# Attention and feed-forward in one kernel: the order of each engine's queue written down as a table

## The chip, the cores and the metric

The kernel runs on one core of one Trainium2 chip. The metric is the device time of one launch in microseconds (us). Before the change it was 1242.29 us, the median of three runs (1240.87 to 1242.33).

## The reference, cut to what matters

Attention over 8 batches of 8 heads, 576 tokens, 64 columns a head, with a block-causal mask of 64x64 blocks. Its output is reshaped to 4608 tokens of 512 columns and goes through a feed-forward part with a hidden width of 2048:

```python
scores = scale * np.matmul(q, k.transpose(0, 1, 3, 2))      # scale = 1/8
scores = np.where(block_i >= block_j, scores, -1000000000.0)
attn = softmax(scores);  x = attn @ v  ->  (4608, 512)
h = x @ w_in                                                 # 512 x 2048
g = np.where(h >= 1, h, np.where(h <= -1, 0.0, (h + 1) ** 2 / 4))
out = g @ w_out                                              # 2048 x 512
```

All inputs and the output are float32.

## The kernel before, in words

**Precision.** Nearly every operand of TensorE is split into a high and a low word of a rounded float32 format, and a product is the sum of three matmuls (high by high, high by low, low by high). That is why one `ffn_in` issues 12 matmuls (L777) and one `ffn_out` 12 (L801, L806), and why the scores are two matmuls a tile (L484 and L487), where the tiles `ka`/`qa` and `kb`/`qb` hold both words. `ka` and `qa` also hold four rows that make the mask; these are written by VectorE into a small tile `mrow` (L134 to L138) and sent into `qa` and `ka` by four DMAs (L150, L151).

**Attention.** There are 32 pairs (batch, two heads). A pair is a generator of eight steps; a step issues one group of scores (`scores`, `scores_last`), the turning of an earlier group of probabilities (`turn`), a piece of the product with v (`attn_v`), and a piece of the next pair's preparation. A group of scores is: matmuls into a PSUM bank `ps_s` (L484, L487); a row maximum on VectorE (`nm`, L508; L533 and L537 for the last group); the exponential on ScalarE (L513, L539); one over the sum on VectorE (`sm`, L494, L495); a multiplication on VectorE (`pr`, L519; L548 for the last group). `turn` then transposes the probabilities on TensorE (L559 or L561, into `ps_t`), in the first batch straight from `pr`, later from a copy that a DMA makes (L247, L251), which here lies in unused ends of `xl` or `vsr`. The next pair's q and k are split on VectorE and GpSimd (`qs` L353 and L354, `ks` L365 and L366) and transposed (L424) in the first two batches; later pairs take another path (L403).

**Weights.** The two weight matrices come in 32 pieces of 512 KB into tiles `bits` (L165) and are split by a helper `convert`: two operations on ScalarE (L170, L171), three on VectorE (L172, L175, L178), one on GpSimd (L184), one on ScalarE (L186), one on GpSimd (L188). `w_in` stays in SBUF, `w_out` goes back to memory in split form.

**Feed-forward.** Nine chunks of 512 tokens by 16 slices of 128 hidden columns. Its steps begin after 36 attention steps, one for each further attention step, and run alone at the end. A slice is 12 matmuls into the only bank `ph` (L777), the activation on ScalarE and VectorE (L786, L787, L790), the split of g (L791 on ScalarE, L792 on GpSimd), and 12 matmuls into four banks `po` (L801, L806).

**What sets the order.** The program text says which step issues what, and each tile comes from a pool that hands out its buffers in turn (3 banks `work`, 1 `ph`, 4 `po`; 2 or 3 buffers for most SBUF tiles, 6 for the small ones). The order in which the instructions stand in the queue of each engine, and in that of the SP queue which issues the DMAs, is decided by the ordering tool when the program is built. An engine then takes its queue strictly from the front: an instruction that waits holds up all that stand behind it.

## Time and profile before

| | |
|---|---|
| median of three runs | 1242.29 us |
| the profiled execution | 1239.06 us |
| its span, first to last instruction | 1237.3 us |
| TensorE busy | 1186.6 us, 96% |
| VectorE busy | 863.8 us, 70% |
| ScalarE busy | 698.5 us, 56% |
| GpSimd busy | 371.8 us, 30% |
| mean granted TensorE clock | 0.989 |

The profiled execution is 3.2 us (0.26%) under the median. In the rows of the profile PE is TensorE, PEld its weight loads, DVE VectorE, ACT ScalarE, POOL GpSimd and SPq the queue that issues DMAs. A row of a timeline is: start in us, duration, engine, line, operation, output<-inputs, shape; in brackets the idle time of the engine ahead of it and what ended that. A row of a stretch is: the stretch, its length, the busy time and the instructions of each engine, the granted TensorE clock (1.00 is full rate, 0.50 half), the DMA share and GB/s.

### The profile page before, as it was taken

The page shows a single profiled execution, that of the slowest core. Times are in us where ns is not written, and L with a number is a line of the kernel's source. Part 1 is how long each engine was busy: PE and PEld are TensorE (multiplying, and loading weights), DVE is VectorE, ACT ScalarE, POOL GpSimd, SP SyncE. Part 2 cuts the span into 40 slices and gives each one's busy share as a digit, 9 for nine tenths or more (in the row PEclk, how much of TensorE's full clock was granted, in tenths as well). Part 3 has the DMA queues.
Part 4 walks back from the last instruction along what each step waited for, and adds up shares of the span by engine and source line. Part 5 has one row for each costly group of instructions (what it writes and reads, how often), then busy time and mean ns, then how long its engine had stood idle before and what let it go on. Part 6 is the DMA issues. An engine that isn't in the chain of part 4 may idle for free.

```text
span 1237.3 us, 19822 instructions
## 1 busy us (share of the span) xinstructions
PE 1186.6 (96%) x6280; PEld 993.1 (80%) x6280; DVE 863.8 (70%) x2124; ACT 698.5 (56%) x1731; POOL 371.8 (30%) x366
## 2 busy tenths in 40 slices
PE   4878898999999999999999999999999999999998
PEld 3666677788888888888888888888888888888886
DVE  8888778658777877787777877787778776322322
ACT  5877667546566656665666665666566654222222
POOL 3444546312222222222222222222222222222222
PEclk9988998999999999999999999999999999999999
DMA  5756776778986655565555555565556443333332
GB/s 165 213 176 208 235 247 221 225 202 255 291 270 219 192 162 156 147 198 166 163 159 180 164 160 160 148 196 151 155 149 192 142 135 111 119 102 102 120 103 102
DMA packets 177192, 215.40 MB, mean 174 GB/s; under 512 B 109872, under 2 KB 128304, under 8 KB 176320
## 3 DMA queue, kind: packets, MB, share of 16 engines
q1 hardware_dynamic: 177088, 214.14, 56.1%
q8 instruction: 50, 0.82, 0.3%
q14 instruction: 54, 0.44, 0.1%
HBM read 134.74 MB, written 31.98 MB: 135 GB/s over the span
## 4 chain that ended last, share of the span: by engine, by line
PE 86%; DVE 5%; DMA 4%; ACT 2%; issue 2%; POOL 1%; SPq 0%; ACTq 0%; DVEq 0%; POOLq 0%
PE ph L777 31%; PE po L801 20%; PE po L806 10%; PE ps_av L598 9%; PE ps_s L484 5%; PE ps_s L487 4%; PE ps_t L559 4%; PE ps_qk L403 1%; DMA bits<-in_moe_w_in_dram 1%; DVE bits L172 1%; POOL bits L184 1%; PE ps_t L561 1%; DVE nm L508 1%; DVE bits L178 1%; DVE shifted L175 1%
## 5 line engine op out<-in xcount | busy, mean ns | idle before, releaser
L792 POOL TENSOR_TENSOR gl<-t,gh 128x512 fp32r<-128x512 f32 x144 | 186.5, 1295 | 522.8 <-ACT gh L791 338.2
L801 PE MATMUL po<-wo,gh 128*128 128x512 f32 x1152 | 294.1, 396 | 0.1
L801 PEld LDWEIGHTS po<-wo,gh 128*128 128x128 f32 x1152 | 211.2, 188 | 43.3 <-ACT gh L791 0.6
L777 PE MATMUL ph<-xh,wih 128*128 128x512 f32 x576 | 232.7, 404 | 0.4 <-DVE t L790 0.4
L777 PE MATMUL ph<-xh,wil 128*128 128x512 f32 x576 | 228.1, 396 | 0.0
L777 PE MATMUL ph<-xl,wih 128*128 128x512 f32 x576 | 226.9, 394 | 0.0
L787 DVE SCALAR_TENSOR_TENSOR t<-t 128x512 f32<-128x512 f32 x144 | 101.0, 701 | 161.5 <-ACT t L786 158.6
L786 ACT ACTIVATE t<-ph 128x512 f32<-128x512 f32 x144 | 86.2, 599 | 160.5 <-PE ph L777 160.5
L791 ACT CAST gh<-t 128x512 fp32r<-128x512 f32 x144 | 89.4, 621 | 118.9 <-DVE t L790 118.8
L806 PE MATMUL po<-wo,gl 128*128 128x512 f32 x576 | 155.3, 391 | 0.0
L484 PE MATMUL ps_s<-ka,qa 68*128 68x288 f32 (+4 forms) x384 | 133.8, 363 | 4.9 <-DMA ka<-mrow 4.0
L513 ACT ACTIVATE pr<-ps_s,nm 128x128 f32<-128x128 f32 x192 | 100.4, 525 | 57.5 <-DVE nm L508 56.4
L508 DVE TENSOR_REDUCE nm<-ps_s 128x1 f32<-128x128 f32 (+3 forms) x256 | 118.9, 482 | 16.4 <-PE ps_s L487 15.6
L777 PEld LDWEIGHTS ph<-xh,wil 128*128 128x128 f32 x576 | 109.1, 189 | 24.0
L806 PEld LDWEIGHTS po<-wo,gl 128*128 128x128 f32 x576 | 108.0, 188 | 22.9
L777 PEld LDWEIGHTS ph<-xl,wih 128*128 128x128 f32 x576 | 109.6, 190 | 19.3
L777 PEld LDWEIGHTS ph<-xh,wih 128*128 128x128 f32 x576 | 109.2, 190 | 19.3 <-DVE t L790 0.8
L381 POOL TENSOR_TENSOR vsr<-vn,vsr 64x64 fp32r<-64x64 f32 (+1 forms) x96 | 56.5, 589 | 227.1 <-ACT vsr L380 226.0
L487 PE MATMUL ps_s<-kb,qb 128*128 128x288 f32 (+4 forms) x384 | 120.4, 321 | 0.0
L790 DVE TENSOR_TENSOR t<-ph,t 128x512 f32<-128x512 f32 x144 | 98.7, 685 | 2.0
L559 PEld LDWEIGHTS ps_t<-ident_r,prr 128*128 128x128 f32 x600 | 68.5, 139 | 22.4 <-issue 0.5
L494 DVE TENSOR_SCALAR sm<-sm 128x1 f32<-128x1 f32 x256 | 38.5, 151 | 65.0 <-ACT pr L513 54.8
(115 smaller groups left out, 1879.7 us busy)
## 6 DMA issues: line engine op xcount, KB each, us to landing
wo<-wo_split SPq DMA_DIRECT2D x144, 512.0 KB, 3.4
prr<-pr SPq DMA_DIRECT2D x96, 192.0 KB, 3.0
prr<-pr SPq DMA_DIRECT2D x48, 256.0 KB, 2.8
out_dram<-ob SPq DMA_DIRECT2D x36, 256.0 KB, 2.9
bits<-in_moe_w_in_dram SPq DMA_DIRECT2D x16, 512.0 KB, 4.6
bits<-in_moe_w_out_dram SPq DMA_DIRECT2D x16, 512.0 KB, 4.0
wo_split<-ws SPq DMA_DIRECT2D x16, 512.0 KB, 2.9
qa<-qb SPq DMA_DIRECT2D x63, 128.0 KB, 2.4
```

Of the source, the lines that this page charges most:

```text
L484: nc.tensor.matmul(ps, qa[:KA, j, c0 : c0 + P], ka[:KA, j, k0 : k0 + n], start=first, stop=False)
L487: nc.tensor.matmul(ps, qb[:, j, c0 : c0 + P], kb[:, j, k0 : k0 + n], start=False, stop=last)
L508: nc.vector.tensor_reduce(out=nm[:, i : i + 1], in_=ps[:, cs], axis=AX.X, op=ALU.max, negate=True)
L513: nc.scalar.activation(raw[:, cs], ps[:, cs], AF.Exp, bias=nm[:, i : i + 1], scale=1.0, accum_out=sm[:, i : i + 1],)
L559: nc.tensor.transpose(out.bitcast(F32R), src, ident_r)
L598: nc.tensor.matmul(ps[:, lo_col:], vt, x, start=first and i == 0 and m == 0, stop=last and i == len(parts) - 1 and m == len(mov) - 1,)
L777: nc.tensor.matmul(ph, w[:, cc, fs], x[:, cc, xs], start=(cc == 0 and i == 0), stop=(cc == NCC - 1 and i == 2),)
L787: nc.vector.scalar_tensor_tensor(out=t_, in0=t_, scalar=1.0, in1=t_, op0=ALU.min, op1=ALU.mult)
L790: nc.vector.tensor_tensor(out=t_, in0=ph, in1=t_, op=ALU.max)
L792: nc.gpsimd.tensor_tensor(out=gl, in0=t_, in1=gh.bitcast(F32), op=ALU.subtract)
L801: nc.tensor.matmul(po[tt], gh[:, ts_], wo[:, w, :], start=(fc == 0 and w == 0), stop=False)
L806: nc.tensor.matmul(po[tt], gl[:, ts_], wo[:, 0, :], start=False, stop=fc == NFC - 1)
```

## The change

Two things are written into the program as tables. `SLOTS` names the buffer that each tile gets: pools have one buffer for each tag, and a helper `slot` adds the next digit of the table to the tag, so that the buffers "t0" and "t1" stand for what were two buffers of "t". `QUEUES` holds, for each of the five queues, a list of numbers (packed and written as text). At the end of the kernel all instructions of an engine are put into the order of its list, and a dependence without a semaphore is laid from each to the next, which fixes the order:

```diff
+SLOTS = {
+    "nat": (
+        '0210210210210210210210210210210210210210'
+    ),
...
+QUEUES = {
...
+    "Pool": (
+        'c-qa6;SPWx2!uhz)%(A29AZ$v-3pe(xATxr2)<ADvqg#}Q8$Jvp5RM^UQ6Fh+no&iPNRp_=?tDO8n>lPpDHQd<lf7j<A2pu='
...
-    att2 = ctx.enter_context(tc.tile_pool(name="att2", bufs=3))
+    att2 = ctx.enter_context(tc.tile_pool(name="att2", bufs=1))
...
+    turns = {tag: iter(x) for tag, x in SLOTS.items()}
+
+    def slot(pool, shape, dtype, tag, name):
+        return pool.tile(shape, dtype, tag=tag + next(turns[tag]), name=name)
...
-            pr = att3.tile([P, S], F32, tag="pr", name="pr")
+            pr = slot(att3, [P, S], F32, "pr", "pr")
...
+    emitted = [
+        x for x in nc.cur_bb.bb.instructions
+        if not isinstance(x, (mybir.BassTilePoolBoundary, mybir.InstRegisterMove))
+    ]
+    for engine, table in QUEUES.items():
+        left = [x for x in emitted if str(x.engine).rsplit(".", 1)[-1] == engine]
+        queue = [left.pop(n) for n in array("H", zlib.decompress(base64.b85decode(table)))]
+        for before, after in zip(queue, queue[1:]):
+            tc.add_manual_dep(
+                after, before.name,
+                mybir.DependencyInfo(mybir.DependencyClass.NoSync, mybir.DependencyReason.DATA),
+                reason="queue",
+            )
```

The instructions are the same ones on every engine: 6170 on TensorE, 2126 on VectorE, 1413 on ScalarE, 371 on GpSimd, 952 in the SP queue. Which tile shares a buffer with which is also the same, up to the buffers' names. Only the order differs, and only in the front part of each queue: on TensorE among the first 1808 instructions (1524 of them stand at another place, none further than 35 places up or 26 down), on VectorE among the first 785 (540 moved, up to 13 places), on ScalarE among the first 524 (397), on GpSimd among the first 156 (95), in the SP queue among the first 412 (369, up to 39 places). In the trace of before this is about the first 400 us. The lines of the changed kernel are numbered anew: its L484 is now L597, L487 L600, L777 L890, L559 L672, L424 L537, L365 L478, L172 L285, L508 L621, L519 L632, L787 L900, L790 L903, L165 L278, L150 and L151 L263 and L264, L336 and L341 L449 and L454, L317 and L320 L430 and L433. Three places are shown; the numbers behind the names tell tiles of one name apart.

**The SP queue at the start.** `qn` and `kn` are q and k of the first pair, `vs` its v, `bits` pieces of the weights, `mrow` the rows of the mask. Before, from the row of k's last blocks on:

```order
L341 DMA kn<-in_k_dram 64x64 x2
L317 DMA vs<-in_v_dram 128x4x64
L320 DMA vs<-in_v_dram 64x64
L317 DMA vs<-in_v_dram 128x4x64
L320 DMA vs<-in_v_dram 64x64
L165 DMA bits<-in_moe_w_in_dram 128x1024 x2
L150 DMA qa<-mrow 4x576
L151 DMA ka<-mrow 4x576
L150 DMA qa<-mrow 4x576
L151 DMA ka<-mrow 4x576
```

In the changed kernel, from the same row on:

```order
L454 DMA kn<-in_k_dram 64x64 x2
L278 DMA bits<-in_moe_w_in_dram 128x1024 x2
L264 DMA ka<-mrow 4x576
L263 DMA qa<-mrow 4x576
L454 DMA qn<-in_q_dram 64x64
L433 DMA vs<-in_v_dram 64x64 x2
L548 DMA qa<-qb 64x512
L278 DMA bits<-in_moe_w_in_dram 128x1024
L449 DMA qn<-in_q_dram 128x2x256
L263 DMA qa<-mrow 4x576
L548 DMA ka<-kb 64x512
```

The four loads of v moved behind the weights and behind the mask rows of the first head, and the mask rows of the second head moved further back.

**TensorE at about 125 us.** `ph_1514` is a slice of the feed-forward, `ps_t_1450` the transposes of a group of probabilities that a DMA has put into `xl`. Before:

```order
L424 MATMUL ps_qk_1396<-ident_r_92,ks_1317 128x128 x4
L777 MATMUL ph_1514<-xh_94,wih_96 128x512
L484 MATMUL ps_s_1438<-ka_103,qa_101 128x512
L487 MATMUL ps_s_1438<-kb_104,qb_102 128x512
L777 MATMUL ph_1514<-xl_95,wih_96 128x512
L777 MATMUL ph_1514<-xh_94,wil_97 128x512
L559 MATMUL ps_t_1450<-ident_r_92,xl_95 128x128 x3
```

In the changed kernel:

```order
L537 MATMUL ps_qk_1396<-ident_r_92,ks_1317 128x128
L597 MATMUL ps_s_1438<-ka_103,qa_101 128x512
L890 MATMUL ph_1514<-xl_95,wih_96 128x512
L890 MATMUL ph_1514<-xh_94,wil_97 128x512
L600 MATMUL ps_s_1438<-kb_104,qb_102 128x512
L890 MATMUL ph_1514<-xh_94,wih_96 128x512
L890 MATMUL ph_1514<-xl_95,wih_96 128x512
L890 MATMUL ph_1514<-xh_94,wil_97 128x512
L672 MATMUL ps_t_1450<-ident_r_92,xl_95 128x128 x3
```

Three more matmuls of `ph_1514` now stand ahead of the transposes.

**VectorE at about 185 us.** `ks_2229` is a later pair's k, `bits_2083` a piece of the weights, `nm_2119`, `sm_2120` and `pr_2118` one group of probabilities, `t_2103` a slice's activation. Before:

```order
L354 SCALAR_TENSOR_TENSOR qs_2192<-qn_2184,qs_2192 128x9x64
L365 CAST ks_2229<-kn_2188 128x8x64
L365 CAST ks_2229<-kn_2188 128x64
L634 TENSOR_TENSOR xl_95<-ps_av_2066,xh_94 128x320
L172 TENSOR_SCALAR bits_2083<-bits_2083 128x512
L175 TENSOR_SCALAR shifted_202<-bits_2083 128x512
L178 SCALAR_TENSOR_TENSOR bits_2083<-bits_2083,shifted_202 128x512
L787 SCALAR_TENSOR_TENSOR t_2103<-t_2103 128x512
L508 TENSOR_REDUCE nm_2119<-ps_s_2117 128x1
L790 TENSOR_TENSOR t_2103<-ph_2090,t_2103 128x512
```

In the changed kernel:

```order
L478 CAST ks_2229<-kn_2188 128x8x64
L467 SCALAR_TENSOR_TENSOR qs_2192<-qn_2184,qs_2192 128x9x64
L572 CAST ka_103<-ps_qk_2057 64x2x64
L285 TENSOR_SCALAR bits_2083<-bits_2083 128x512
L288 TENSOR_SCALAR shifted_202<-bits_2083 128x512
L291 SCALAR_TENSOR_TENSOR bits_2083<-bits_2083,shifted_202 128x512
L747 TENSOR_TENSOR xl_95<-ps_av_2066,xh_94 128x320
L621 TENSOR_REDUCE nm_2119<-ps_s_2117 128x1
L900 SCALAR_TENSOR_TENSOR t_2103<-t_2103 128x512
L903 TENSOR_TENSOR t_2103<-ph_2090,t_2103 128x512
```

The short cast `ks_2229` of 128x64 is no longer in this stretch: it stands 13 places earlier in the queue, right behind the two L632 of `pr_1984`; and the row maximum `nm_2119` has moved ahead of L900.

## The prediction

> **What bounds the kernel now.** I read the page's busy times first, then the busy time in five stretches, and after that the chain of waits and the timeline at the places of TensorE's waits. The stretches come early because the change reaches only the front part of the queues.

> ```profile
> PE 1186.6 (96%) x6280; PEld 993.1 (80%) x6280; DVE 863.8 (70%) x2124; ACT 698.5 (56%) x1731; POOL 371.8 (30%) x366
> ```

> ```profile
> 0.00:20.00 20.00, 5.61 (x28) 4.73 (x29) 14.28 (x42) 8.56 (x19) 5.09 (x12) 1.00 0.66 191
> 20.00:70.00 50.00, 40.41 (x224) 32.73 (x222) 46.56 (x130) 40.24 (x104) 24.36 (x22) 1.00 0.62 188
> 70.00:150.00 80.00, 66.88 (x338) 53.52 (x339) 62.98 (x166) 57.05 (x144) 37.78 (x35) 0.87 0.67 206
> 150.00:250.00 100.00, 92.72 (x466) 73.78 (x465) 74.52 (x167) 63.74 (x148) 46.94 (x42) 0.97 0.73 232
> 250.00:1236.00 986.00, 981.03 (x5230) 828.37 (x5228) 665.47 (x1623) 528.87 (x1319) 257.61 (x256) 1.00 0.54 165
> ```

> TensorE bounds the whole. Its idle time is 20 - 5.61 = 14.4 us in the first stretch, then 9.6, 13.1 and 7.3, and from 250 us on 986 - 981.03 = 5.0. The work stays the same, so a new order can gain only from the 44.4 us of idle before 250 us, from a few of the last 5, and from the granted clock, which is 0.87 and 0.97 in two stretches. From 20 to 70 us VectorE is busy 46.56 of 50: there it sets the pace, and a better order of TensorE alone brings little.

> The clock falls in steps of about 3.4 us. These are stretches cut on that grid:

> ```profile
> 87.25:90.66 3.41, 2.30 (x16) 1.57 (x14) 3.38 (x10) 1.56 (x5) 0.21 (x2) 1.00 0.62 165
> 90.66:94.07 3.41, 1.00 (x6) 0.69 (x6) 2.58 (x8) 2.55 (x10) 2.32 (x2) 1.00 0.22 49
> 94.07:97.48 3.41, 1.59 (x10) 1.57 (x10) 3.41 (x12) 2.28 (x7) 2.31 (x2) 0.50 0.77 249
> 97.48:100.89 3.41, 3.41 (x14) 2.74 (x13) 2.32 (x9) 3.17 (x8) 1.55 (x2) 0.50 0.80 282
> 124.80:128.20 3.40, 0.77 (x6) 0.36 (x4) 2.07 (x4) 1.88 (x4) 0.80 (x1) 1.00 0.89 324
> 128.20:131.62 3.42, 3.42 (x13) 2.74 (x12) 1.15 (x4) 1.83 (x4) 1.28 (x2) 0.50 0.75 246
> 189.65:193.06 3.41, 1.67 (x11) 1.35 (x9) 2.29 (x6) 1.58 (x4) 2.22 (x2) 1.00 0.92 322
> 193.06:196.47 3.41, 2.44 (x8) 2.06 (x9) 2.38 (x7) 2.03 (x5) 1.66 (x2) 0.50 0.40 123
> 196.47:199.88 3.41, 3.41 (x11) 2.64 (x9) 2.71 (x6) 2.63 (x7) 1.50 (x2) 0.50 0.70 267
> ```

> Each spell at half rate follows a stretch in which TensorE was busy 1.67 of 3.41 us or less; the one with 2.30 was followed by none. The rate stays at half until a stretch was full (97.48, 128.20, 196.47). So a wait costs its own length, and then half of the time of the work that runs slowly.

> **The change part by part.** Buffers are shared as before, so the slot table costs nothing by itself. What counts is which waits stand ahead of which work, and I follow the places where TensorE waits.

> *The start.* The first scores wait for the mask rows in `ka`. Pieces of the chain, then of the timeline:

> ```profile
> 8.71 4.84 DMA ka<-mrow
> 13.69 0.45 PE ps_s L484
> ```

> ```profile
> 4.28 0.59 SPq L317 DMA_DIRECT2D vs<-in_v_dram  x1
> ...
> 6.66 1.06 SPq L165 DMA_DIRECT2D bits<-in_moe_w_in_dram  x2
> ...
> 9.23 0.69 DVE L431 CAST ka<-ps_qk 64x512 fp32r<-64x512 f32 x1
> ...
> 13.40 0.68 ACT L170 ACTIVATE bits<-bits 128x512 f32<-128x512 f32 x1 [1.08 <-DMA bits<-in_moe_w_in_dram]
> ```

> `ka<-mrow` landed at 8.71 + 4.84 = 13.55, right behind the second piece of the weights (13.40); both were issued after the loads of v. In the changed queue the weights begin where those loads stood, 6.66 - 4.28 = 2.4 us sooner, and VectorE fills `mrow` ahead of the splits of k. The first scores should begin at 13.69 - 2.4 = 11.3. They can't begin before L431 ends, 9.23 + 0.69 = 9.92, a gain of 3.8; and nothing is gained if the mask rows land no sooner. VectorE runs nearly full from there to 70 us, and L285 on a piece of weights now stands ahead of the first row maxima, so of the 2.4 I keep 2.0. The moved loads of v and the second head's mask rows are first used several microseconds after they now land. Bounds: 0 and 3.8.

> *27 to 74 us.* VectorE's rows are exchanged among themselves, some weight operations out of the way of a group of probabilities, some into it. I take 0, by bounds of 1 on both sides, the length of one or two of them.

> *92, 110 and 125 us.* Three waits of TensorE, each with what stands behind it:

> ```profile
> 95.89 1.30 PE L561 MATMUL ps_t<-ident_r,pr 128*128 128x128 f32 x5 [2.94 <-DVE sm L494]
> 96.84 0.81 PE L424 MATMUL ps_qk<-ident_r,ks 128*128 128x128 f32 x4
> 97.46 0.76 PE L484 MATMUL ps_s<-ka,qa 68*128 68x512 f32 x1
> ```

> ```profile
> 112.09 0.45 PE L559 MATMUL ps_t<-ident_r,xl 128*128 128x128 f32 x3 [1.45 <-DMA xl<-pr]
> 112.37 0.37 PE L484 MATMUL ps_s<-ka,qa 68*128 68x288 f32 x1
> 112.58 0.30 PE L487 MATMUL ps_s<-kb,qb 128*128 128x288 f32 x1
> 112.72 0.30 PE L484 MATMUL ps_s<-ka,qa 68*128 68x288 f32 x1
> ```

> ```profile
> 128.00 0.49 PE L559 MATMUL ps_t<-ident_r,xl 128*128 128x128 f32 x3 [2.63 <-ACT ps_s L513]
> ...
> 128.84 0.63 PE L777 MATMUL ph<-xl,wih 128*128 128x512 f32 x1
> 129.26 0.63 PE L777 MATMUL ph<-xh,wil 128*128 128x512 f32 x1
> ```

> At 92 us the changed queue puts the four L424 ahead of the L561 that wait: 97.46 - 96.84 = 0.6 us of work goes into the wait. On VectorE one weight operation leaves the way of the probabilities that are waited for, and others enter it; the next group's L519 comes ahead of a row maximum. I take 1.0; bounds 0 and the wait, 2.9. At 110 us two of the L484 and one L487 go ahead of the wait for the copied probabilities, 112.72 - 112.37 = 0.35 for two, 0.4 in all; bounds 0 and 1.45. At 125 us it is three L777, which start 129.26 - 128.84 = 0.42 apart at half rate: 3 x 0.42 = 1.3. TensorE's busy time in 124.80 to 128.20 goes from 0.77 to about 1.5 at full rate, still under 1.67, so I leave the spell at half rate behind it in place. If it goes too, another 3.42 / 2 = 1.7 is gained: bounds 0 and 3.0.

> *190 us.* TensorE, then VectorE, with the same pair of casts from the start for comparison:

> ```profile
> 194.03 0.62 PE L559 MATMUL ps_t<-ident_r,xl 128*128 128x128 f32 x3 [2.71 <-DVE pr L519]
> ```

> ```profile
> 5.51 0.62 DVE L365 CAST ks<-kn 128x512 fp32r<-128x512 f32 x2
> ...
> 181.14 0.43 DVE L172 TENSOR_SCALAR bits<-bits 128x512 f32<-128x512 f32 x1 [1.56 <-ACT bits L170]
> ...
> 184.71 2.25 DVE L365 CAST ks<-kn 128x512 fp32r<-128x512 f32 x2
> ...
> 189.86 0.68 DVE L787 SCALAR_TENSOR_TENSOR t<-t 128x512 f32<-128x512 f32 x1
> ```

> The wait of 2.71 ends with `pr_2118`, and the chain to it on VectorE begins with two casts that take 2.25 instead of 0.62, 1.6 more. The short one now stands in front of L172 where VectorE was idle 1.56, and the row maximum no longer waits for L787 (0.68). The chain comes 1.6 + 0.6 = 2.2 us sooner, and one L777 goes ahead of the wait. What is left of the 2.71 is 0.3 or so; the stretch is then busy over 2.30, and the spell at half rate should go: (2.44 + 3.41) / 2 = 2.9. Together 5.1, of which later waits, whose chains come only 2.2 sooner, take back part: I take 3.0; bounds 0 and 5.1. [...]

> *From 250 us.* TensorE is full, and some score matmuls are moved up as far as 21 places, ahead of others, although their bank comes free only with an exponential. Such a wait lasts at most about a row maximum and an exponential:

> ```profile
> L513 ACT ACTIVATE pr<-ps_s,nm 128x128 f32<-128x128 f32 x192 | 100.4, 525 | 57.5 <-DVE nm L508 56.4
> L508 DVE TENSOR_REDUCE nm<-ps_s 128x1 f32<-128x128 f32 (+3 forms) x256 | 118.9, 482 | 16.4 <-PE ps_s L487 15.6
> ```

> 0.525 + 0.482 = 1.0 us for each. I charge one, 1.0; bounds: all of the idle time of 5.0 gained, or the loss of the slower rival below.

> The sum: 2.0 + 0 + 1.0 + 0.4 + 1.3 + 3.0 - 1.0 = 6.7 us gained. The profiled execution would go from 1239.06 to 1232.4; it is 3.2 us under the median, so against the median of 1242.29 I forecast 1242.29 - 6.7 = 1235.6. A change of 0.2% (2.5 us) is about what a measurement of this kernel can tell from none.

> **The rivals.**

> *Given back, no change (0.17).* VectorE is busy 46.56 of 50 us before 70 us, so an earlier start may only become a longer wait for it, and the waits after 200 us may eat the rest: of the terms only 0.4 + 1.3 would stay, less 1.0: 0.7 gained, 1241.6. For it: VectorE's share. Against it: that share falls to 62.98 of 80 behind 70 us, and at 125 and 190 us VectorE stood idle too.

> *Slower, by new waits in the full part (0.13).* Each pair has one L444; from 250 to 400 us there are five, the first and the last at

> ```profile
> 259.15 0.22 PE L444 MATMUL ps_qk<-ident_r,qk 128*128 128x128 f32 x1
> ...
> 393.97 0.25 PE L444 MATMUL ps_qk<-ident_r,qk 128*128 128x128 f32 x1
> ```

> If in each pair three groups of scores wait 1.0 us, 15 us of TensorE's time is new idle; against gains of 6.7 + 1.0 = 7.7 that is 7.3 us lost, 1249.6. It decides from 7.7 + 2.5 = 10.2 us of new idle behind 250 us. For it: the strict order, and only 5.0 us of waits there now, which the change can hardly better. Against it: most of the moves are within work that is all ready.

> *Larger, because half rate goes nearly everywhere (0.12).* If the waits at 90.66 and 124.80 also shrink until their stretches are busy over 2.30, the spells behind them vanish: (1.59 + 3.41) / 2 + 3.42 / 2 = 4.2 more, and with the full 5.1 instead of 3.0 at 190 us, 2.1 more: 13.0 gained, 1229.3. Against it: what moves into those waits is 0.6 and 1.3 us.

> *The clock doesn't follow the waits (0.10).* If the rate falls for another cause, the spell behind 190 us stays; that term is then 2.2 at most, I take 1.5, and the sum is 5.2: 1237.1. For it: at 87.25 a stretch with 1.1 us of idle was not followed by half rate, so the length of a wait isn't all. Against it: the rows at 90.66, 124.80 and 189.65, each followed at once by 0.50. [...]

> My forecast has what is left, 0.48. Faster by over 0.2% are the forecast, the third and the fourth: 0.48 + 0.12 + 0.10 = 0.70. Within 0.2% is the first, 0.17, and slower the second, 0.13. The range leaves out the slower rival and a little of the larger one: from 1227, two below it for its bounds at the start, to 1243, where the no-change case ends with its own 1.4 us of play.

> **What would show it.** In the changed kernel's profile: the first L597 at 11.3 instead of 13.69; at about 190 us no stretch at 0.50 and a wait of under 1 us ahead of L672; at 125 us a wait of 1.3 to 2; the two L478 at 0.62 together, or 2.25 elsewhere. Busy TensorE time from 250 us to the end of its span should leave 5 to 7 us idle. The prediction is wrong if the idle there is over 10 us, if VectorE in the first 70 us is as busy and ends as late as before, or if half rate comes at places where it was 1.00 before.

## The result, and the profile after

The changed kernel took 1232.54 us (median of five runs, 1230.39 to 1235.36), the kernel before 1240.87 in the five runs counted with it. The ratio is 0.9936 (95% interval 0.9914 to 0.9959), 7.9 us less; 6.7 was forecast. The profiled execution after, 1235.36 us, is the slowest of its five, so its trace shows a smaller gain than the runs do.

The busy times and the stretches of the changed kernel, columns as before:

```profile
PE 1192.4 (97%) x6280; PEld 990.8 (80%) x6280; DVE 856.2 (69%) x2124; ACT 696.2 (56%) x1731; POOL 371.1 (30%) x366
```

```profile
0.00:20.00 20.00, 8.66 (x40) 7.39 (x40) 16.58 (x50) 10.89 (x24) 6.46 (x13) 1.00 0.64 181
20.00:70.00 50.00, 43.53 (x229) 34.67 (x228) 44.60 (x133) 41.93 (x112) 24.55 (x23) 0.97 0.70 205
70.00:150.00 80.00, 72.53 (x384) 56.38 (x383) 67.83 (x181) 61.16 (x150) 41.27 (x35) 0.96 0.74 228
150.00:250.00 100.00, 96.46 (x483) 74.58 (x484) 68.30 (x160) 60.86 (x146) 44.05 (x42) 1.00 0.77 235
250.00:400.00 150.00, 148.19 (x806) 122.86 (x805) 113.89 (x288) 88.89 (x232) 39.33 (x44) 1.00 0.77 236
400.00:1232.00 832.00, 823.07 (x4348) 694.92 (x4346) 544.97 (x1319) 432.46 (x1071) 215.46 (x211) 1.00 0.48 149
```

TensorE's idle time up to 250 us fell from 44.4 to 11.3 + 6.5 + 7.5 + 3.5 = 28.8 us, and the granted clock from 70 to 150 us rose from 0.87 to 0.96. At 250 us the instructions of TensorE run some 16 us sooner than the same ones in the trace of before (the median over those matched one to one), part of which is other work put off. At the end of the trace only 3.7 us are left (span 1233.6 against 1237.3). Up to there the gain is larger than forecast, and much of it is lost again: TensorE is idle for 1.8 + 8.9 = 10.7 us between 250 and 1232 us, where 5 to 7 were forecast. The largest single loss is one wait. TensorE's row, then the stretches on the clock's grid:

```profile
410.00 0.59 PE L672 MATMUL ps_t<-ident_r,prr 128*128 128x128 f32 x3 [3.88 <-DMA prr<-pr]
```

```profile
406.02:409.44 3.42, 0.10 (x1) 0.00 (x0) 0.90 (x4) 0.00 (x0) 0.00 (x0) 1.00 0.97 364
409.44:412.85 3.41, 2.85 (x14) 2.88 (x14) 1.68 (x3) 1.00 (x2) 1.09 (x1) 0.50 0.22 83
412.85:416.26 3.41, 3.41 (x12) 2.83 (x13) 2.29 (x4) 1.74 (x4) 0.50 (x2) 0.50 0.90 292
```

A wait of 3.9 us for copied probabilities, with two stretches at half rate behind it: 3.9 + (2.85 + 3.41) / 2 = 7.0 us, where the kernel before had no wait at all.

The start, in TensorE's and the SP queue's timeline:

```profile
10.59 0.48 PE L597 MATMUL ps_s<-ka,qa 68*128 68x128 f32 x1 [0.90 <-DVE ka L544]
...
16.21 0.61 PE L597 MATMUL ps_s<-ka,qa 68*128 68x288 f32 x1 [2.90 <-DVE ka L572]
```

```profile
4.25 1.06 SPq L278 DMA_DIRECT2D bits<-in_moe_w_in_dram  x2
5.91 0.76 SPq L264 DMA_DIRECT2D ka<-mrow  x1
```

The first scores begin at 10.59 instead of 13.69, and what they wait for is no longer the mask rows but VectorE's copy into `ka`. At 190 us of before, now about 178, the wait of 2.71 is down to this:

```profile
178.09 0.40 PE L597 MATMUL ps_s<-ka,qa 68*128 68x288 f32 x1 [0.50 <-ACT pa L665]
```

### The profile page after: what moved, and what is told of

The parts are those of the page before. It is cut to its first block, busy times and chain, and to the rows that moved or that the text cites. A ratio compares the mean times of both kernels' runs of the same rounds, so it can differ in the third digit from the quotient of the medians.

```text
span 1233.6 us, 19821 instructions
## 1 busy us (share of the span) xinstructions
PE 1192.4 (97%) x6280; PEld 990.8 (80%) x6280; DVE 856.2 (69%) x2124; ACT 696.2 (56%) x1731; POOL 371.1 (30%) x366
## 4 chain that ended last, share of the span: by engine, by line
PE 87%; DVE 5%; DMA 3%; ACT 2%; issue 1%; POOL 1%; SPq 0%; ACTq 0%; DVEq 0%; POOLq 0%
PE ph L890 31%; PE po L914 20%; PE po L919 10%; PE ps_av L711 10%; PE ps_s L597 5%; PE ps_s L600 4%; PE ps_t L672 4%; PE ps_qk L516 1%; PE ps_t L674 1%; DVE pr L632 1%; DMA xl<-pr 1%; DVE nm L621 1%; ACT ps_s L626 1%; DVE bits L285 1%; DMA vsr<-pr 1%
## 5 line engine op out<-in xcount | busy, mean ns | idle before, releaser
L914 PE MATMUL po<-wo,gh 128*128 128x512 f32 x1152 | 315.5, 398 | 2.1 <-DMA wo<-wo_split 1.6
L890 PE MATMUL ph<-xh,wih 128*128 128x512 f32 x576 | 232.5, 404 | 1.9 <-DVE sm L607 1.2
L890 PE MATMUL ph<-xh,wil 128*128 128x512 f32 x576 | 229.3, 398 | 0.0
L890 PE MATMUL ph<-xl,wih 128*128 128x512 f32 x576 | 227.6, 395 | 0.0
L900 DVE SCALAR_TENSOR_TENSOR t<-t 128x512 f32<-128x512 f32 x144 | 100.8, 700 | 163.3 <-ACT t L899 159.0
L919 PE MATMUL po<-wo,gl 128*128 128x512 f32 x576 | 169.6, 394 | 0.0
L597 PE MATMUL ps_s<-ka,qa 68*128 68x288 f32 (+4 forms) x384 | 134.0, 363 | 7.7 <-DVE ka L572 3.3
L621 DVE TENSOR_REDUCE nm<-ps_s 128x1 f32<-128x256 f32 (+3 forms) x256 | 118.3, 482 | 17.9 <-PE ps_s L600 16.6
L890 PEld LDWEIGHTS ph<-xh,wih 128*128 128x128 f32 x576 | 108.6, 189 | 23.0 <-DVE t L903 2.3
L890 PEld LDWEIGHTS ph<-xh,wil 128*128 128x128 f32 x576 | 108.6, 188 | 22.8
L890 PEld LDWEIGHTS ph<-xl,wih 128*128 128x128 f32 x576 | 108.8, 189 | 19.6 <-DVE xl L747 0.2
L600 PE MATMUL ps_s<-kb,qb 128*128 128x288 f32 (+4 forms) x384 | 122.0, 328 | 0.0
L494 POOL TENSOR_TENSOR vsr<-vn,vsr 64x64 fp32r<-64x64 f32 (+1 forms) x96 | 55.1, 577 | 211.7 <-ACT vsr L493 208.7
L903 DVE TENSOR_TENSOR t<-ph,t 128x512 f32<-128x512 f32 x144 | 98.7, 685 | 2.3
L672 PEld LDWEIGHTS ps_t<-ident_r,prr 128*128 128x128 f32 (+1 forms) x600 | 69.2, 139 | 26.1 <-issue 5.9
L597 PEld LDWEIGHTS ps_s<-ka,qa 68*128 68x128 f32 x384 | 73.8, 193 | 18.0 <-DVE ka L572 4.4
```

The costliest lines, as they stand in the source:

```text
L597: nc.tensor.matmul(ps, qa[:KA, j, c0 : c0 + P], ka[:KA, j, k0 : k0 + n], start=first, stop=False)
L600: nc.tensor.matmul(ps, qb[:, j, c0 : c0 + P], kb[:, j, k0 : k0 + n], start=False, stop=last)
L621: nc.vector.tensor_reduce(out=nm[:, i : i + 1], in_=ps[:, cs], axis=AX.X, op=ALU.max, negate=True)
L672: nc.tensor.transpose(out.bitcast(F32R), src, ident_r)
L890: nc.tensor.matmul(ph, w[:, cc, fs], x[:, cc, xs], start=(cc == 0 and i == 0), stop=(cc == NCC - 1 and i == 2),)
L900: nc.vector.scalar_tensor_tensor(out=t_, in0=t_, scalar=1.0, in1=t_, op0=ALU.min, op1=ALU.mult)
```

## The experiments

My theory was that single waits of TensorE make the gain, each worth about what stands in its row, and that the full part behind 250 us loses about 1 us. The rivals: the lead is given back at the next wait; new waits behind 250 us eat the gain; the tables do something of their own. Twelve kernels were run, on three chips. Ratios are to the kernel before on the same chip, with 95% intervals; 0.1% is 1.24 us.

| kernel | ratio | interval |
|---|---|---|
| old_order | 1.0006 | 0.9993 to 1.0019 |
| start_only | 0.9978 | 0.9969 to 0.9987 |
| ve185_only | 0.9996 | 0.9986 to 1.0006 |
| pe190_only | 1.0013 | 1.0000 to 1.0026 |
| pe125_only | 0.9985 | 0.9976 to 0.9994 |
| to70 | 0.9979 | 0.9966 to 0.9992 |
| to120 | 0.9897 | 0.9874 to 0.9921 |
| to285 | 0.9874 | 0.9853 to 0.9894 |
| to370 | 0.9951 | 0.9933 to 0.9968 |
| changed kernel | 0.9936 | 0.9914 to 0.9959 |
| sp_tail | 0.9930 | 0.9912 to 0.9948 |
| ve_55_125 | 1.0067 | 1.0050 to 1.0085 |
| pe_55_125 | 1.0049 | 1.0031 to 1.0067 |

**The tables without the order.** `QUEUES` holds the order of before, `SLOTS` stays:

```diff
 for engine, table in QUEUES.items():
-    queue = changed[engine]
+    queue = old[engine]
```

> Both tables are in the program, but the queue table holds the order that the tool had given before. My theory (the order alone does it): the time of before, a ratio of 1.000 within 0.2%. Rival (the tables, the named buffers or the dependences laid by hand cost or save something of themselves): over 0.2% away from it, up to the whole 8 us.

No difference, so everything below is the order's. Its trace also shows what one trace is worth: with the same order, its instructions run up to 2.4 us later than in the trace of before.

**The start alone.** The order of before, with these moves:

```diff
 SP      kn<-in_k_dram
+        bits<-in_moe_w_in_dram x2, ka<-mrow, qa<-mrow (first head)
         vs<-in_v_dram x4
-        bits<-in_moe_w_in_dram x2, qa<-mrow, ka<-mrow (first head)
 VectorE
+        msel
         qs<-qn 128x8x64
-        msel
+        mrow<-msel x2
         qs<-qn 128x64
```

> The order of before but for the start: the two weight pieces and the first head's two mask rows go ahead of the four loads of v in the SP queue, and VectorE writes the mask rows ahead of the rest of q's split. Theory: the first scores begin 2 to 3 us sooner, and 2 us of that last to the end: 1239 against 1241. Rival (VectorE sets the pace up to 70 us, so the head start becomes a longer wait there): the first scores begin as early, but by 80 us nothing is left, and the time is that of before within 0.1%.

0.22% is 2.7 us. TensorE at the start of this kernel:

```profile
10.72 0.45 PE L597 MATMUL ps_s<-ka,qa 68*128 68x128 f32 x1 [0.39 <-DVE ka L544]
...
17.77 0.47 PE L674 MATMUL ps_t<-ident_r,pr 128*128 128x128 f32 x1 [4.36 <-DVE pr L632]
```

The first scores come 3 us sooner; the next wait ends at 17.77 (before: idle from 16.37 for 3.23, so 19.60), 1.8 us sooner. By the times most of the lead lasts, as the theory had it. The trace does not show it lasting: it is of the slowest of the twelve runs, and from 60 us on its instructions run at most 0.8 us sooner or later than in the trace of before.

**One wait of TensorE filled, at 125 us.** The order of before, but

```diff
 TensorE
+        ph_1514 x3
         ps_t_1450 x3
-        ph_1514 x3
```

> The order of before but for three matmuls of ph_1514 on TensorE, ahead of the transposes ps_t_1450 that wait at 125 us. Theory: 1.3 us gained, or 3.0 if the spell at half rate behind it goes too: 1238 to 1240. Rival (VectorE and the copied probabilities are what is late, so the next wait grows by as much): the time of before within 0.1%.

0.15% is 1.9 us, between the theory's two figures. The wait, and the stretch behind it:

```profile
127.57 0.51 PE L672 MATMUL ps_t<-ident_r,xl 128*128 128x128 f32 x3 [1.92 <-ACT ps_s L626]
```

```profile
124.31:127.73 3.42, 1.50 (x8) 0.94 (x7) 1.99 (x4) 1.91 (x5) 0.85 (x1) 1.00 0.86 310
127.73:131.14 3.41, 3.08 (x13) 2.55 (x13) 1.23 (x4) 2.07 (x4) 2.02 (x2) 0.50 0.72 249
```

Here the wait is 1.92 instead of 2.63 and the spell at half rate stayed, as the prediction had worked it out (busy 1.5 of 3.4). The length of this wait in a single trace proves little, though: in the other traces with the order of before there it is 2.22 to 2.58, and in that of pe190_only only 0.99, with no half rate behind it. What these three matmuls are worth rests on the times.

**The wait at 190 us, from either side.** First two instructions of VectorE, then TensorE's rows from 186 to 200 us alone, all else as before:

```diff
 VectorE  pr_1984 x2
+         ks_2229 128x64
 ...
          ks_2229 128x8x64
-         ks_2229 128x64
 ...
+         nm_2119
          t_2103
-         nm_2119
```

> The order of before but for two instructions of VectorE: the short cast of ks_2229 right behind pr_1984, and the row maximum nm_2119 ahead of the activation of t_2103. Theory: the wait of 2.7 us at 191 us falls under 1 us, no spell at half rate follows, and 3 to 5 us are gained: 1237. Rival (GpSimd holds up whichever VectorE operation it meets, or later waits take it back): the wait stays over 2 us or moves on, under 1.5 us gained.

```diff
-queue["PE"] = old["PE"]
+queue["PE"] = old["PE"][:676] + sorted(old["PE"][676:721], key=changed["PE"].index) + old["PE"][721:]
```

> The order of before on every queue, but TensorE's instructions that stood between 186 and 200 us stand among themselves as in the changed kernel: score matmuls ahead of feed-forward matmuls, one ph matmul and two po groups behind them. The run with VectorE's two moves alone left a wait of 1.9 us there and gained nothing. Theory: the score matmuls start the chain on VectorE sooner and the feed-forward matmuls fill the wait: it falls from 2.7 to under 1 us, no half rate behind it, 2 to 4 us gained. Rival (the lead of 0.5 to 2 us meets later waits at 213 and 218 us and is given back): under 1 us gained.

Neither gained. In the first, the time that the casts lost before is lost elsewhere, again with GpSimd at work. VectorE, GpSimd and TensorE of that kernel:

```profile
177.79 1.28 DVE L478 CAST ks<-kn 128x64 fp32r<-128x64 f32 x1
...
185.93 1.53 DVE L288 TENSOR_SCALAR shifted<-bits 128x512 uint32<-128x512 uint32 x1
```

```profile
177.73 1.29 POOL L301 TENSOR_TENSOR ws<-bits,ws 128x512 fp32r<-128x512 f32 x1 [0.61 <-DMA bits<-in_moe_w_in_dram]
...
185.57 1.60 POOL L479 TENSOR_TENSOR ks<-kn,ks 128x576 fp32r<-128x576 f32 x1
```

```profile
191.96 0.45 PE L672 MATMUL ps_t<-ident_r,xl 128*128 128x128 f32 x3 [1.86 <-DVE pr L632]
```

The short cast starts 0.06 us behind a GpSimd operation of 1.29 and takes 1.28 instead of 0.2 (before, 63.03: 0.18), ending 0.05 us behind it. The long cast is now quick, 0.41, but L288 starts 0.36 us behind the next GpSimd operation, of 1.60, and takes 1.53 instead of 0.43 (before, 188.79), ending 0.29 us behind it. The prediction counted the casts' 1.6 us as gained; here the short cast and L288 lose 1.1 each, and nothing of the term is left. The changed kernel shows the same: its two casts take 0.48 and 0.62, but L285 at 167.10 starts 0.09 us behind a GpSimd operation of 1.32 and takes 1.52, ending 0.29 us behind it. Why they take so long is not shown; the rows show only where they stand to GpSimd's operations. In the second, TensorE waits twice:

```profile
188.62 0.50 PE L890 MATMUL ph<-xh,wih 128*128 128x512 f32 x1 [1.30 <-DVE t L903]
...
190.85 0.37 PE L672 MATMUL ps_t<-ident_r,xl 128*128 128x128 f32 x2 [1.27 <-DVE pr L632]
```

The `ph` matmul that was moved ahead waits for L903, which VectorE reaches too late in its old order. One wait of 2.71 became two of 1.3.

**Where along the queues the gain lies.** Four kernels with the changed order up to a cut and the order of before behind it. The cut takes the first instructions of TensorE (238, 462, 1204, 1656, one more each than the expectations count) and on the other queues what these need:

```diff
-queue[e] = changed[e]
+head = changed[e][:cut[e]]
+queue[e] = head + [x for x in old[e] if x not in head]
```

> The changed order for the first 237 instructions of TensorE (up to about 70 us of the changed kernel) and all that they need, the order of before behind it. Theory (each shorter wait counts where it stands): the 4 to 6 us by which TensorE leads at 70 to 80 us in the two profiles stay, 1236. Rival (the lead is given back at the next wait): under 2 us gained, 1239 or more.

> The same with the first 461 instructions of TensorE (up to about 123 us). Theory: TensorE leads by 9 to 12 us at that place in the two profiles; some of that is work put off, so 7 to 9 us gained, 1233. Rival (given back at the next wait): as the run to 70 us, 1236 or more.

> The same with the first 1203 instructions of TensorE (up to about 285 us): the waits of 0.4 to 0.8 us behind 285 us and the one of 3.9 us at 406 us of the changed kernel's profile are left out. Theory (the changed order wins 11 to 15 us up to there and gives 4 to 8 back behind it): 1227 to 1230. Rival (the wait at 406 us was an accident of that one execution, not of the order): the changed kernel's own median, 1232.5.

> The changed order for the first 1655 instructions of TensorE (up to about 370 us of the changed kernel) and all that they need, the order of before behind it. The run with the changed order up to 285 us took 1223.5, the changed kernel 1232.5. Theory (the loads of q and k that stand ahead of the copy at 406 us make most of the loss): no wait over 1 us near 406 us, 1224 to 1227. Rival (the loss is spread over small waits between 285 and 370 us): 1229 or more.

By the times, the kernel cut at 70 us gains 2.6 us, no more than the start alone. The one cut at 120 us gains another 0.82%, 10 us, and the one cut at 285 us another 0.23%, 2.9 us (within the intervals' width). Cut at 285 us, the kernel takes 1223.45 us (1222.16 to 1224.80), by the ratios 15.6 us less than before: the fastest version found. Behind 285 us the changed order loses 0.62%, 7.7 us.

These differences are not the worth of each stretch alone, because a cut can cost something itself: behind it the old order asks for results that the new one has put off. The kernel cut at 70 us shows it. TensorE in the kernel before, then in this one:

```profile
68.97 0.63 PE L561 MATMUL ps_t<-ident_r,pr 128*128 128x128 f32 x4 [2.10 <-DVE pr L519]
...
72.49 1.30 PE L561 MATMUL ps_t<-ident_r,pr 128*128 128x128 f32 x5 [2.54 <-DVE sm L494]
...
75.68 1.90 PE L598 MATMUL ps_av<-pa,vs 128*128 128x256 f32 x6
...
80.31 2.17 PE L598 MATMUL ps_av<-pb,vs 128*128 128x320 f32 x8
```

```profile
68.86 0.82 PE L711 MATMUL ps_av<-pa,vs 128*128 128x256 f32 x4
71.67 0.70 PE L711 MATMUL ps_av<-pa,vs 128*128 128x256 f32 x2 [2.00 <-ACT pa L665]
...
76.17 0.48 PE L597 MATMUL ps_s<-ka,qa 68*128 68x128 f32 x1 [2.24 <-DMA ka<-kb]
...
78.90 2.90 PE L711 MATMUL ps_av<-pb,vs 128*128 128x320 f32 x8
```

The waits of before at 67 and 70 us are gone from it, and the product with `pa` begins 6.8 us sooner (69.62 in the changed kernel). Then come two waits that neither full order has, with half rate from 73.56 to 80.38 us, and the product with `pb` begins only 1.4 us sooner (5.8 in the changed kernel, at 74.50). So up to the cut the order gains about as much as in the changed kernel, and the cut itself gives most of it back; some of the 10 us that the next cut gains is this loss left out.

The traces show where the gain arises. The lead is how much sooner TensorE's instructions start than the same ones in the trace of before: the median, in us, of those that start in each stretch of before, matched by line, operands and order, without the score matmuls, which can't be matched so.

| us of before | changed | cut at 70 | cut at 120 | cut at 285 | cut at 370 |
|---|---|---|---|---|---|
| 60 to 70 | 1.5 | 2.3 | 1.4 | 1.6 | 1.1 |
| 70 to 80 | 6.2 | 6.0 | 6.1 | 6.3 | 4.9 |
| 80 to 90 | 5.5 | 0.4 | 5.2 | 5.6 | 4.0 |
| 110 to 120 | 9.1 | 3.5 | 8.8 | 9.1 | 6.7 |
| 130 to 140 | 11.8 | 3.5 | 11.2 | 12.3 | 9.5 |
| 180 to 190 | 12.5 | 3.5 | 10.8 | 13.1 | 10.1 |
| 200 to 210 | 16.1 | 3.2 | 11.1 | 16.6 | 14.3 |
| 280 to 290 | 15.9 | 2.8 | 10.2 | 17.6 | 15.3 |
| 360 to 370 | 11.7 | 2.6 | 10.2 | 16.4 | 11.2 |
| 420 to 430 | 4.1 | 2.8 | 10.3 | 16.5 | 6.5 |

The lead grows in steps at the places where before waits (67 and 70, 92 to 112, 125 and 190 us), by about the same amount in each kernel that has the changed order there. One step is not the order's alone: from 80 to 120 us the kernel cut at 70 gains 3.1 us too, with the order of before. Behind 285 us the lead falls by more than 1.2 us only in the kernels that go on with the changed order.

The full part in the kernel cut at 285, then in the changed one:

```profile
285.00:370.00 85.00, 84.77 (x475) 72.29 (x474) 65.50 (x168) 52.17 (x137) 24.21 (x28) 1.00 0.87 277
370.00:430.00 60.00, 59.92 (x333) 50.76 (x332) 47.59 (x120) 37.46 (x97) 16.44 (x18) 1.00 0.60 183
```

```profile
285.00:370.00 85.00, 83.50 (x455) 69.38 (x454) 64.84 (x163) 49.94 (x131) 22.04 (x25) 1.00 0.78 243
370.00:430.00 60.00, 55.56 (x291) 46.64 (x290) 42.60 (x106) 33.62 (x87) 15.85 (x18) 0.94 0.64 190
```

From 285 to 370 us the changed order gets 20 matmuls fewer done, although the busy time differs by only 1.3 us: most of the loss does not show as idle time. The lead falls by 4.2 us there, against 1.2 in the kernel cut at 285. Two waits show, of which the longer is for the `qa` that VectorE writes (the other, of 0.46 at 301.87, for its `pb`); the kernel cut at 285 and that of before have none:

```profile
287.94 0.37 PE L597 MATMUL ps_s<-ka,qa 68*128 68x288 f32 x1 [0.82 <-DVE qa L561]
```

From 370 to 430 us it is the wait at 406.

The run cut at 370 went against the theory: 1232.95, no better than the changed kernel. It has lost 4.1 us of lead from 285 to 370 us as well, and then a wait of its own just behind the cut, with a stretch at half rate:

```profile
375.90 0.54 PE L672 MATMUL ps_t<-ident_r,prr 128*128 128x128 f32 x3 [3.05 <-DVE pr L632]
```

So it can't tell what the wait at 406 us is worth.

**The wait at 406 us.** In the changed kernel's SP queue, loads of a later pair's q and k (`qk`, and the copies that they read, `rawq` and `rawk`), which before were issued from 395.0 to 399.3 us, 11 to 16 us ahead of that copy (410.64), stand right in front of it:

```profile
400.53 0.60 SPq L412 DMA_DIRECT2D qk<-rawk  x1
401.17 0.63 SPq L416 DMA_DIRECT2D qk<-rawq  x1
401.84 0.61 SPq L412 DMA_DIRECT2D qk<-rawq  x1
402.57 0.54 SPq L907 DMA_DIRECT2D wo<-wo_split  x1
403.20 0.49 SPq L364 DMA_DIRECT2D prr<-pr  x1
```

The copy issued at 403.20 is what the wait ends on, 6.8 us later at 410.00. So the SP queue got the order of before behind its 354th place:

```diff
-queue["SP"] = changed["SP"]
+queue["SP"] = changed["SP"][:354] + [x for x in old["SP"] if x not in changed["SP"][:354]]
```

> The changed kernel with one queue altered: the SP queue has the changed order for its first 354 places and the order of before behind it, so that the loads of q and k of a later pair no longer stand right ahead of the copy of the probabilities that TensorE waits for at 406 us. Theory (the order of these DMAs makes the wait): no wait over 1 us near 406 us, no half rate there, 1227 to 1231. Rival (an accident of the execution, or another late DMA takes its place): 1232 or more.

The wait at 406 went: the same copy, issued at 402.65, landed in 3.2 us instead of 6.7. In its profile no stretch behind 113 us is at half rate. But two shorter waits took its place:

```profile
351.83 0.47 PE L914 MATMUL po<-wo,gh 128*128 128x512 f32 x1 [1.63 <-DMA wo<-wo_split]
```

```profile
391.79 0.34 PE L672 MATMUL ps_t<-ident_r,prr 128*128 128x128 f32 x2 [0.92 <-DMA prr<-pr]
```

The time, 1230.74 (ratio 0.9930), can't be told from that of the changed kernel. That the postponed loads make the copy late fits both profiles with a long wait; shown is only that another order of the SP queue from there moves the wait. Whether the wait of 3.9 us is there in each execution stays open.

**VectorE or TensorE.** What makes the gain between 55 and 125 us? The rows that stood there, in the changed order on one engine at a time:

```diff
-queue["DVE"] = old["DVE"]
+queue["DVE"] = old["DVE"][:131] + sorted(old["DVE"][131:298], key=changed["DVE"].index) + old["DVE"][298:]
```

> The order of before on every queue, but VectorE's instructions that stood between 55 and 125 us stand among themselves as in the changed kernel. The two runs with the changed order up to 70 and up to 120 us differ by 10 us, far more than the terms that I had given to that stretch. Theory now: VectorE's order makes it, because row maxima and divisions no longer queue behind weight operations: the waits of 2.1 and 2.5 us at 66 to 72 and of 1.5 and 2.9 at 90 to 96 shrink by half, 5 us or more gained. Rival one (TensorE's order makes it, by filling the waits): under 2 us gained here. Rival two (only the two together): under 2 us gained here and in the run with TensorE's order alone.

```diff
-queue["PE"] = old["PE"]
+queue["PE"] = old["PE"][:158] + sorted(old["PE"][158:431], key=changed["PE"].index) + old["PE"][431:]
```

> The counterpart: the order of before on every queue, but TensorE's instructions that stood between 55 and 125 us stand among themselves as in the changed kernel. Theory (VectorE's order makes the gain): under 2 us gained, or a loss, since new instructions stand in front and VectorE is no sooner. Rival one (TensorE's order): 5 us or more gained. Rival two (only together): under 2 us.

My theory, that VectorE's order does it, falls: VectorE's part alone is 0.67% slower than before, TensorE's part 0.49% slower. The stretch of 70 to 150 us with VectorE's order alone, with TensorE's alone, and with the whole changed order up to 120 us:

```profile
70.00:150.00 80.00, 64.60 (x310) 50.51 (x311) 56.23 (x160) 53.66 (x136) 31.73 (x29) 0.79 0.57 175
```

```profile
70.00:150.00 80.00, 63.01 (x311) 49.34 (x312) 58.48 (x166) 55.80 (x141) 35.73 (x31) 0.85 0.62 196
```

```profile
70.00:150.00 80.00, 72.45 (x381) 56.33 (x379) 67.70 (x178) 61.94 (x152) 41.47 (x37) 0.96 0.74 228
```

With one engine's order changed, both engines are busy less than before (66.88 and 62.98) and the clock is lower; with all five, both are busy more. Each engine takes its queue from the front: the three `ph_1514` matmuls that in before stand behind the wait of 2.63 us at 125 us start at 128.28 us, after it, and put ahead of it (pe125_only) they start at 124.80. If only one engine asks for results in the new order, it waits for the others in the old order. With VectorE's order alone, VectorE waits for ScalarE's exponentials, 2.52 us at 76.63 and 2.23 at 79.86, where the longest wait of before between 55 and 80 us is 0.82; with TensorE's alone, TensorE still waits for VectorE, 2.14 at 71.69 and 1.47 at 75.22 (before: 2.10 and 2.54). A kernel with just these two parts together was not run, so how much the other three queues add is open.

## Why the prediction was nearly right, and where its steps were not

The direction, the size and the range held, but the sum did so by luck: two errors cancelled. Up to 285 us the order gains 15.6 us, where the terms had 7.7; behind it 7.7 are lost, where the sum had 1.0. Two of the three signs by which the prediction called itself wrong came. The idle time from 250 us on is 10.7 us, over its limit of 10. Half rate comes at 409 us, where before had full rate (that at 47.62 us is also new, but old_order has it too, at 51.74, so it need not be the change's). Of the remaining sign half came: VectorE is as busy in the first 70 us, 61.2 us against 60.8, but with 183 instructions instead of 172.

- *The start, 2.0.* Right: 2.7 measured (interval 1.6 to 3.8), the first scores sooner than thought (10.59 against 11.3).
- *27 to 74 us, 0.* This is the step that failed most. The lead grows there from 1.5 to 6.2 us, by 3.7 to 4.7 in each kernel with the changed order: the waits of 2.10 and 2.54 us shrink or go, and with them the half rate that before has from 70.17 to 77.00 us. The prediction names neither wait; it priced the stretch by single operations of VectorE. The two half changes show why that fails: the orders of the engines act together, and one engine's part alone costs 6 to 8 us.
- *92 and 110 us, 1.0 + 0.4.* Too small as it looks: the lead grows by 3.6 us from 80 to 120 us. But 3.1 come in the kernel cut at 70 too, so the order's share is not shown.
- *125 us, 1.3.* Right for the three matmuls: 1.9, interval 0.7 to 3.0, the spell at half rate staying. In the changed kernel more changed: the wait is 0.73 where 1.3 to 2 was forecast, and no half rate follows.
- *190 us, 3.0.* The size was about right, its making was not. The lead grows by 3.6 us there (3.5 in the kernel cut at 285, 0.3 in the one cut at 120, which has the order of before there). But the two moves on VectorE, from which the term was worked out, gain nothing alone (0.9996), since the short cast and L288 take 1.1 us more each beside GpSimd's operations, and TensorE's rows alone gain nothing either (1.0013).
- *From 250 us, a loss of 1.0.* That new waits come in the full part was right, the size and the kind were not: 7.7 are lost behind 285 us. The prediction's score matmuls that wait for their bank show in no row. What shows is the wait for a copy by DMA, 3.88 us and the half rate behind it, and two waits for VectorE, 0.82 and 0.46. The prediction judged the SP queue by when data is needed, not by what is issued right ahead of a copy that TensorE waits for (landed 6.7 us after its issue, against 3.2 in sp_tail). The rival with new waits in the full part needed 10.2 us of new idle; in this trace there are 10.7 - 5.0 = 5.7, and 3.1 more are lost to half rate. What makes the rest of the loss stays open.

Of the rivals, "given back" is refuted by the kernels cut at 120 and 285 us, which keep their lead to the end; what the kernel cut at 70 gives back it loses to its cut. "Half rate goes nearly everywhere" was half right: up to 450 us the trace of before has 27.3 us at half rate from 36 us on, the changed kernel's 17.1, 6.8 of these at 409, and the kernel cut at 285 has 10.2 us. "The clock doesn't follow the waits" is settled in the last section: it follows them, on a grid.

## What to carry to other kernels

An order of queues is one thing across all engines: don't price it wait by wait, and don't try it one engine at a time, since half of a good order was slower than none of it here, by 0.67 and 0.49%. Cut it along time instead, with the old order behind the cut: that showed that the last part of the table costs half of the gain. But a cut makes waits of its own, as those at 70 and 370 us did, so look at the trace right behind it before reading its time. Where the bound engine is already full, the new order gained nothing here and lost 7.7 us, DMAs that nobody waits for included: leave it alone there.

## What was not expected of the hardware

```profile
193.44 0.45 PE L672 MATMUL ps_t<-ident_r,xl 128*128 128x128 f32 x3 [2.40 <-DVE pr L632]
```

```profile
189.17:192.58 3.41, 1.88 (x12) 1.52 (x10) 2.29 (x6) 1.69 (x4) 2.33 (x2) 1.00 0.98 308
192.58:196.00 3.42, 2.56 (x13) 2.17 (x14) 2.52 (x7) 2.21 (x7) 1.56 (x2) 1.00 0.50 169
```

In the kernel with VectorE's two moves at 185 us, the shorter wait of 1.86 lies within one stretch, and half rate follows:

```profile
189.07:192.49 3.42, 1.56 (x12) 1.32 (x11) 3.19 (x7) 1.94 (x5) 2.65 (x3) 1.00 0.71 242
192.49:195.90 3.41, 3.41 (x9) 2.63 (x9) 2.47 (x8) 3.41 (x9) 0.71 (x2) 0.50 0.84 287
```

Over the stretches of all fourteen traces from the first record of the clock (at 22 to 38 us) up to 450 us, cut on each trace's own grid, every full-rate stretch with under 1.78 us of busy TensorE was followed by half rate, none with over 2.68; between these both occur. The prediction drew the line at 1.67, from three spells; before has another, from 114.55 to 117.96, behind a stretch that was busy for 2.02, and none behind the stretch from 49.69 that was busy for 2.01. A half-rate stretch was followed by full rate from 2.95 us busy upward and by another at half rate up to 2.88. Half rate came with waits of 1.86 us (ve185_only, 191.96), 1.92 (pe125_only, 127.57), 2.63 and 2.71 (before, 128.00 and 194.03).

Ahead of the first record the views print 1.00, but that is not measured. In the changed kernel two score matmuls of 512 columns start 0.43 us apart at 12.25 us and 0.23 apart at 403.19, where the clock is 1.00; in before, at 0.50, two L777 of 512 columns start 0.42 apart at 128.84. By this spacing TensorE ran at half rate at the start, and the 1.00 of the first two stretches in the prediction can't be relied on.
